# Layer 2's first five tiles scheduled ahead of layer 1's chosen-row MLP

## The chip, the cores and the metric

The kernel runs on one core of one Trainium2 chip. The metric is the device time of one execution in microseconds, as the median of several runs. Beside it stands one profiled execution, whose trace is what every row below is taken from.

## The reference

Two identical layers run one after the other on x of shape 2048 x 512 (bf16). Each layer adds a sliding-window attention and then a "mixture of depths" step that runs an MLP for a single row:

```python
x = x + A(layernorm(x))
    # qkv = x @ wqkv (512 x 1536); 32 heads of 16; query i sees keys i-255..i
    # p = softmax(q k^T / 4, masked);  (p @ v) @ wo (512 x 512)
x = x + B(layernorm(x))
    # r = x @ w_r                  one score per row, 2048 of them
    # idx = the row with the largest r (C = 1)
    # y = (silu(x[idx] @ w_gate) * (x[idx] @ w_up)) @ w_down   (512->1792->512)
    # y = y * sigmoid(r[idx]);  row idx gets + y, every other row gets + 0
    # B returns x + that update
```

So layer 2 differs from a plain second pass in one row only, and which row that is is known only when all rows of layer 1 are done. Attention looks backward alone: a query needs keys of at most 255 rows before it. With the inputs of this case the reference picks row 1105 in layer 1 (score 4.315; the next is row 1082 with 4.040). In tiles of 128 rows both lie in tile 8.

## The kernel before

The 2048 rows are 16 tiles of 128. For every tile `ln_tile` normalises (bn_stats on DVE, the rest on POOL), a DMA transpose turns the tile (`transpose`; PE does it for tiles 0 and 1 of a layer), and `proj` makes q, k and v in PSUM bank 7 (`BK_PR`), from which DVE copies them. `attend` runs eight head groups: scores on PE into banks 0 to 2 or 3 to 5 (L665, and L684 for a mask), one exp on ACT (L696; tile 0 of a layer has smaller ones, L691 and L693), an edge mask on POOL (L706, L710), and the product with v on PE into bank 6 (L725). `norm_half` divides, `out_tile` multiplies with wo in bank 7 (L750), adds the residual and calls `mod_tile`, which makes the row statistics and the score r.

After tile 15 `mod_global` finds the largest score over all rows: reductions on DVE, two matmuls with an identity (L818, L820) that turn a column into a row, a copy of the chosen tile by ACT with an index read from memory (`pick`, L836, L837), a gather by PE (L842, L844), gate and up on PE (224 matmuls, L866), silu on ACT and DVE, down on PE (L882), and the scaled result in YBC (L885). Layer 2 starts with `upd_tile` (L912): for each of its tiles DVE adds YBC times a one-hot column to the 128 rows, which changes at most one row of one tile.

No engine order is written by hand. A list scheduler (`Sched`) simulates the five engines with a cost for each operation and a priority, and emits each engine's instructions in the order so found, with semaphores. `Fast.build` gives layer 2 priorities that begin 8 tiles behind layer 1's, and each of its tiles reads what `mod_global` wrote. `warm` adds matmuls of the lowest priority (L907) that the scheduler puts where PE has nothing else: 60 after layer 1, 40 after layer 2. All users of bank 7 keep the order in which the program adds them.

At the end every engine loads a flag (L1111) that tells whether an exp over- or underflowed, and branches (L1112): the code of a slow safe version (`Safe`) lies between the branch and the end of the program. SP then waits for all DMAs (L322).

Of the kernel before, what the change touches and what calls it, by code (L numbers as in the profile page):

```python
# [57 lines left out]
class _Op:  # L58
    __slots__ = ("idx", "eng", "fn", "deps", "dur", "name", "is_dma", "prio", "signals", "count",
                 "dma_sem", "start", "end", "waits", "dma_extra", "soft")  # L60

    def __init__(self, idx, eng, fn, deps, dur, name, is_dma, prio):
# [15 lines left out]
        self.soft = ()  # L78


class Sched:
    ENGS = ("pe", "act", "dve", "pool", "sp")

    def __init__(self, dma_latency=1500.0, sem_latency=120.0, n_dma_slots=40):
# [8 lines left out]
        self._vc_lookup = {}  # L93

    def add(self, eng, fn, reads=(), writes=(), dur=100.0, name="", is_dma=False, prio=None, extra_deps=()):
# [27 lines left out]
        op.soft = soft  # L123
        self.ops.append(op)
# [25 lines left out]
    def schedule(self):  # L150
# [6 lines left out]
        remaining = [len(op.deps) for op in ops]  # L157
        ready_time = [0.0] * n
        now = {e: [] for e in self.ENGS}
        fut = {e: [] for e in self.ENGS}  # L160
        for op in ops:
            if remaining[op.idx] == 0:
                _heappush(now[op.eng], (op.prio, op.idx))
        t_eng = {e: 0.0 for e in self.ENGS}
        order = {e: [] for e in self.ENGS}
        done = 0
        while done < n:
            best = None
            for e in self.ENGS:
# [6 lines left out]
                if nw:  # L176
                    cand = (te, nw[0][0], nw[0][1], e, True)
                elif f:
                    cand = (f[0][0], f[0][1], f[0][2], e, False)
                else:  # L180
                    continue
                if best is None or cand[:3] < best[:3]:
                    best = cand
            st, p, i, e, from_now = best
            if from_now:
                _heappop(now[e])
            else:
                f = fut[e]
                nw = now[e]
                while f and f[0][0] <= st:  # L190
                    rt, p2, i2 = _heappop(f)
                    _heappush(nw, (p2, i2))
                p, i = _heappop(nw)
# [7 lines left out]
            for u in users[i]:  # L201
                remaining[u] -= 1
                rt = op.end + (0.0 if i in ops[u].soft else self.sem_latency)
                if rt > ready_time[u]:
                    ready_time[u] = rt
                if remaining[u] == 0:
                    ue = ops[u].eng
                    if ready_time[u] <= t_eng[ue]:
                        _heappush(now[ue], (ops[u].prio, u))
                    else:  # L210
                        _heappush(fut[ue], (ready_time[u], ops[u].prio, u))
        self.order = order
        self.makespan = max(op.end for op in ops) if ops else 0.0
        self.busy = {e: sum(ops[i].dur for i in order[e]) for e in self.ENGS}

# [80 lines left out]
    def run_engine(self, e, handle, sems, dma_sems):  # L296
        ops = self.ops
        for i in self.order[e]:
# [4 lines left out]
            if op.signals:  # L303
# [4 lines left out]
                else:  # L308
                    last.then_inc(sems[e], 1)

# [28 lines left out]
class Fast:  # L339
    PRE = "f_"  # L340
    RV = 2
    warm0 = 21
    warmn = (60, 40)
# [20 lines left out]
    def alloc(self):  # L364
# [42 lines left out]
        self.IDXS = self.sb("IDXS", [1, 2], I32)  # L407
# [16 lines left out]
    def alloc_attn(self):  # L424
# [8 lines left out]
        self.VSCR = self.nc.dram_tensor(self.PRE + "vscr", [self.SEQ, 544], BF16)  # L433

    def bank(self, b):
        return self.PS[:, b, :]

# [135 lines left out]
    def transpose(self, dst, dk, src, sk, tb):  # L573
# [4 lines left out]
        bb = self.bank(tb).bitcast(BF16)  # L578

        def tr(e):  # L580
# [4 lines left out]
        S.add("pe", tr, reads=sk + ["idb"], writes=["bank%d" % tb], dur=260, name="ptr")  # L585
        S.add("dve", lambda e: e.tensor_copy(out=dst, in_=bb[:, 0:512].rearrange("p (k t) -> p k t", k=4)), reads=[], writes=["bank%d" % tb, dk],  # L586
              dur=430, name="evt")

    def proj(self, L, m, banks=(BK_PR, BK_PR, BK_PR)):
# [13 lines left out]
        def pq(MB=banks[0]):  # L603
            bk = "bank%d" % MB
            for s in range(4):
                S.add("pe", lambda e, s=s: qg(e, MB, 0, s), reads=["xnt%d" % k2, "wqkv0"], writes=[bk], dur=225, name="qproj")
            for h in range(2):
                S.add("dve", lambda e, h=h: e.tensor_copy(out=self.QT[64 * h:64 * h + 64, k2, h],  # L608
                                                          in_=self.bank(MB)[64 * h:64 * h + 64, 0:512].rearrange("p (s t) -> p s t", s=4)),
                      reads=["qz%d" % k2], writes=[bk, "qt%d_%d" % (k2, h)], dur=690, name="evq")  # L610

        def pk(MB=banks[1]):
            bk = "bank%d" % MB
            for s in range(4):
                S.add("pe", lambda e, s=s: qg(e, MB, 1, s), reads=["xnt%d" % k2, "wqkv1"], writes=[bk], dur=225, name="kproj")
# [568 lines left out]
```

## Time and profile before

| | |
|---|---|
| median of 3 runs | 443.31 us (443.02 to 444.98) |
| the profiled execution, its own time | 441.75 us |
| span of the profile, first to last instruction | 440.0 us |
| PE busy | 396.6 us (90%); the filler of L907 is 23.2 us of it |
| DVE, ACT, POOL busy | 299.7, 268.8, 249.6 us |
| mean granted TensorE clock | 0.972 of full speed |

The span leaves out 1.75 us that the execution's own time holds. A busy PE is not the same as a PE that works on the result: the filler of L907 counts as busy. The engines' busy times are averages over two long even stretches (layer 1 and layer 2) and a stretch between them in which the engines take turns.

### The profile page before, as it was taken

What the parts mean: (1) busy time and instruction counts of PE and PEld (TensorE: products, weight loads), DVE (VectorE), ACT (ScalarE), POOL (GpSimd) and SP (SyncE); (2) the same over time, 40 slices, a digit from 0 to 9 for tenths busy, and PEclk for the clock granted to TensorE, in tenths of its full rate; (3) what the DMA queues carried; (4) which work ended last, traced back from release to release, by engine and by line L of the source; (5) the groups of instructions that cost most, each with busy time, mean ns of one, the idle gap of its engine ahead of it and who ended that gap; (6) DMA issues with size and microseconds to landing.
All of it is one profiled execution on the core that took longest, in us unless ns stands there. A gap on an engine that the chain in (4) does not pass through costs nothing.

```text
span 440.0 us, 17737 instructions
## 1 busy us (share of the span) xinstructions
PE 396.6 (90%) x7801; PEld 344.1 (78%) x7861; DVE 299.7 (68%) x740; ACT 268.8 (61%) x280; POOL 249.6 (57%) x468
## 2 busy tenths in 40 slices
PE   6799999999999999999558989999999999999961
PEld 2588888888888888865347878889888988998551
DVE  6899886766666656444489998874875676663730
ACT  1278777777777777830007757777668777779100
POOL 6577666666655555542076666756666555555410
PEclk9899999999999999999969999999999999999985
DMA  8543433333434332210003234222232332221000
GB/s 271 148 87 63 105 73 84 87 85 88 87 88 88 88 80 72 62 37 1 1 12 77 54 52 63 63 65 64 58 71 63 40 68 67 64 54 31 13 16 8
DMA packets 70918, 29.69 MB, mean 67 GB/s; under 512 B 51504, under 2 KB 70832, under 8 KB 70832
## 3 DMA queue, kind: packets, MB, share of 16 engines
q1 hardware_dynamic: 68576, 26.24, 27.3%
q10 hardware_dynamic: 2256, 2.23, 1.6%
q8 instruction: 64, 1.05, 1.1%
q14 instruction: 22, 0.18, 0.2%
HBM read 14.29 MB, written 6.55 MB: 47 GB/s over the span
## 4 chain that ended last, share of the span: by engine, by line
PE 71%; DVE 18%; ACT 4%; DMA 2%; issue 2%; POOL 1%; ACTq 0%; DVEq 0%; POOLq 0%
PE f_PS L665 23%; PE f_PS L725 17%; PE f_PS L599 11%; PE f_PS L750 6%; PE f_PS L907 5%; DVE f_KT L619 4%; PE f_PS L627 4%; DVE f_QT L608 3%; ACT f_PT L696 3%; DVE f_ST L560 2%; DVE f_KTN L616 2%; DVE f_xres L912 1%; PE f_PS L866 1%; PE f_PS L684 1%; DMA f_xin<-in_A_x_dram 1%
## 5 line engine op out<-in xcount | busy, mean ns | idle before, releaser
L696 ACT ACTIVATE f_PT<-f_PS 128x1152 bf16<-128x1152 f32 x240 | 256.4, 1132 | 81.1 <-PE f_PS L665 80.5
L665 PE MATMUL f_PS<-f_QT,f_KT 128*128 128x128 bf16 (+3 forms) x2976 | 173.1, 205 | 7.8 <-ACT f_PT L693 3.2
L665 PEld LDWEIGHTS f_PS<-f_QT,f_KT 128*128 128x128 bf16 x2976 | 145.8, 97 | 25.6 <-ACT f_PT L696 16.7
L706 POOL TENSOR_TENSOR f_PT<-f_PT,f_TM 128x384 bf16<-128x384 bf16 x112 | 102.5, 915 | 87.7 <-ACT f_PT L696 86.8
L725 PE MATMUL f_PS<-f_VBD,f_PT 128*128 128x68 bf16 x2880 | 120.2, 197 | 0.6 <-DVE f_ONORM L739 0.5
L725 PEld LDWEIGHTS f_PS<-f_VBD,f_PT 128*128 128x128 bf16 x2880 | 106.4, 98 | 8.2 <-issue 0.9
L599 PE MATMUL f_PS<-f_XNT,f_wqkv 128*128 128x128 bf16 x1024 | 72.5, 224 | 3.9 <-DVE f_MV L561 2.3
L599 PEld LDWEIGHTS f_PS<-f_XNT,f_wqkv 128*128 128x128 bf16 x1024 | 60.9, 100 | 4.7 <-issue 2.5
L684 PE MATMUL f_PS<-f_BM,f_II 128*128 128x64 bf16 (+1 forms) x256 | 48.8, 191 | 0.0
L737 DVE RECIPROCAL f_RDA<-f_PS 128x16 f32<-128x16 f32 x64 | 15.8, 247 | 47.2 <-PE f_PS L725 46.9
L619 DVE TENSOR_SCALAR f_KT<-f_KTN,f_KM 128x512 bf16<-128x512 bf16 x128 | 46.3, 423 | 0.8
L608 DVE CAST f_QT<-f_PS 64x512 bf16<-64x512 f32 x64 | 44.0, 687 | 4.0 <-PE f_PS L599 1.2
L627 PE MATMUL f_PS<-f_wqkv,f_XNT 128*128 128x512 bf16 x102 | 29.9, 379 | 2.6 <-DVE f_XNT L586 1.3
L750 PE MATMUL f_PS<-f_wo,f_OT 128*128 128x512 bf16 x98 | 26.3, 379 | 5.7 <-DVE f_QT L608 2.2
L691 ACT ACTIVATE f_PT<-f_PS 128x288 bf16<-128x288 f32 x16 | 6.0, 408 | 38.8 <-PE f_PS L665 38.8
L630 DVE CAST f_VN<-f_PS 128x512 bf16<-128x512 f32 x32 | 21.9, 686 | 8.8 <-PE f_PS L627 8.5
L616 DVE CAST f_KTN<-f_PS 128x512 bf16<-128x512 f32 x32 | 22.1, 689 | 8.2 <-PE f_PS L599 8.0
L739 DVE TENSOR_TENSOR f_ONORM<-f_PS,f_RDA 128x256 bf16<-128x256 f32 x64 | 27.0, 421 | 1.0
L684 PEld LDWEIGHTS f_PS<-f_BM,f_II 128*128 128x128 bf16 x256 | 24.5, 96 | 0.0
L772 POOL TENSOR_SCALAR f_RSM<-f_xres 128x1 f32<-128x1 f32 x32 | 8.0, 251 | 28.6 <-DVE f_xres L766 27.8
L562 POOL TENSOR_SCALAR f_MV<-f_MV 128x1 f32<-128x1 f32 x32 | 7.4, 232 | 29.2 <-DVE f_MV L561 26.0
L907 PE MATMUL f_PS<-f_wqkv,f_wo 128*128 128x512 bf16 x97 | 23.2, 379 | 0.2
(125 smaller groups left out, 370.1 us busy)
## 6 DMA issues: line engine op xcount, KB each, us to landing
f_vscr<-f_VN SPq DMA_DIRECT2D x32, 136.0 KB, 2.0
f_VBD<-f_vscr SPq DMA_DIRECT2D x128, 34.0 KB, 2.3
out_dram<-f_OUTB SPq DMA_DIRECT2D x16, 128.0 KB, 1.9
f_xin<-in_B_w_down_dram SPq DMA_DIRECT2D x14, 128.0 KB, 2.3
f_wg<-in_B_w_gate_dram SPq DMA_DIRECT2D x7, 256.0 KB, 3.4
f_wu<-in_B_w_up_dram SPq DMA_DIRECT2D x7, 256.0 KB, 3.6
f_wqkv<-in_A_wqkv_dram ACTq DMA_DIRECT2D x3, 512.0 KB, 5.9
f_xin<-in_A_x_dram SPq DMA_DIRECT2D x1, 1024.0 KB, 10.8
```

The lines of the kernel that those rows point to most:

```text
L599: r = e.matmul(self.bank(MB)[:, 128 * s:128 * s + 128], lhsT=self.wqkv[:, kc, off:off + 128], rhs=self.XNT[:, k2, kc, :], start=(kc == 0), ...
L608: S.add("dve", lambda e, h=h: e.tensor_copy(out=self.QT[64 * h:64 * h + 64, k2, h], in_=self.bank(MB)[64 * h:64 * h + 64, 0:512].rearrange ...
L616: S.add("dve", lambda e: e.tensor_copy(out=self.KTN[:, k2], in_=self.bank(MB)[:, 0:512].rearrange("p (s t) -> p s t", s=4)), reads=[], wri ...
L619: S.add("dve", lambda e, hh=hh: e.tensor_scalar(out=self.KT[:, k4, :, :, hh, :].rearrange("p s b k -> p (s b) k"), in0=self.KTN[:, k2].rea ...
L627: return e.matmul(self.bank(MB)[:, 0:512], lhsT=self.XNT[:, k2, kc, :], rhs=self.wqkv[:, kc, 1024:1536], start=(kc == 0), stop=(kc == 3))
L665: return e.matmul(self.bank(st + k)[:, off:off + n], lhsT=self.KT[:, (b // 4) % 4, s, b % 4].rearrange("p h k -> p (h k)"), rhs=self.QT[:, ...
L684: r = e.matmul(self.bank(st)[:, lo:192], lhsT=self.II[:], rhs=self.BM[:, lo - 128:64], start=False, stop=True, skip_group_check=True)
L696: S.add("act", lambda e: e.activation(out=view, in_=self.PS[:, st:st + 3, 0:384], func=ACTF.Exp, scale=0.25), reads=["ptz%d" % k2], writes ...
L706: S.add("pool", lambda e: e.tensor_tensor(out=w, in0=w, in1=self.TM[:].unsqueeze(1).broadcast_to([128, 6, 2, 32]), op=ALU.mult), reads=["t ...
L725: r = e.matmul(self.bank(BK_PV)[:, c0:c0 + 68], lhsT=self.PT[:, k2, p0:p0 + 128], rhs=self.VBD[:, (b // 4) % 4, b % 4].rearrange("p h (g c ...
L750: return e.matmul(self.bank(MB)[:, 0:512], lhsT=self.OT[:, ko, kc, :], rhs=self.wo[:, kc, :], start=(kc == 0), stop=(kc == 3))
L907: S.add("pe", lambda e: e.matmul(self.bank(5)[:, 0:512], lhsT=self.wo[:, 0, 0:128], rhs=self.wqkv[:, 0, 0:512], start=True, stop=True, ski ...
```

## The change

Layer 2's tiles 0 to 4 (`AHEAD = 5`) no longer read the result of layer 1's MLP: they run on the rows as they stand before the update, and their priorities follow directly on layer 1's. `mod_global(0)` gets a priority amid layer 2's first tiles and uses bank 7 alone, in short pieces (gate and up in halves of seven columns that DVE copies out, down in pieces of four). One dynamic update then changes the chosen row, if it lies in tiles 5 to 15. At that point every engine waits for the update, loads a second flag and branches: if the chosen row lay in tiles 0 to 4, a copy of those tiles, which layer 1 saved to memory, is read back, the update is applied, and all that layer 2 had done so far is done again. The scheduler now chooses the order of bank 7's users itself, each user (matmuls and the copies that read them) being one indivisible turn. The filler after layer 1 is gone. The branch at the end goes through a short block with a hint to its target ahead of it.

```diff
@@ class Sched
+    def trans(self, bank):
+        self.tr_bank.append(bank)
+        self.tr_ops.append([])
+        return len(self.tr_bank) - 1
...
@@ def schedule
+        owner = {b: None for b in self.tr_bank}
+        def blocked(i):
+            t = ops[i].tr
+            return t is not None and owner[self.tr_bank[t]] not in (None, t)
...
+    def cut(self, t):
+        self.cut_at = {}
+        for e in self.ENGS:
+            k = 0
+            while k < len(self.order[e]) and self.ops[self.order[e][k]].start < t:
+                k += 1
+            self.cut_at[e] = k
+
+    def replay(self, first, layer):
+        R = Sched(self.dma_latency, self.sem_latency, 16)
+        first(R)
...
+        keep = sorted((i for i in before if self.ops[i].layer == layer), key=lambda i: (self.ops[i].start, i))
...
@@ class Fast
-    warmn = (60, 40)
+    AHEAD = 5
+    warmn = (0, 40)
+    def hold(self, b):
+        if b != BK_PR:
+            return "bank%d" % b, None
+        t = self.S.trans(b)
+        return "bank%d.%d" % (b, t), t
...
@@ def mod_tile, L == 0
+            if m < self.AHEAD:
+                S.dma("sp", lambda e: e.dma_start(self.XSCR[rows, :], x), reads=[xk], writes=["xscr%d" % m], nbytes=262144, name="x2b", dur=650)
...
@@ def mod_global
+        side = L == 0 and self.AHEAD > 0
+        def place(b):
+            if not side:
+                return self.bank(b), "bank%d" % b, None
+            k, t = self.hold(BK_PR)
+            return self.bank(BK_PR), k, t
...
+        if side:
+            lim = float(self.SEQ - 128 * self.AHEAD - 1)
+            S.add(D, lambda e: e.tensor_scalar(out=self.FLAG[0:1, 1:2], in0=PM[0:1, 3:4], scalar1=lim, scalar2=None, op0=ALU.is_gt), ...
+            S.add(D, lambda e: e.tensor_scalar(out=self.IDXS[0:1, 2:3], in0=self.IDXS[0:1, 1:2], scalar1=self.AHEAD, scalar2=None, op0=ALU.max), ...
+            S.add(D, lambda e: e.tensor_reduce(out=self.OHL[:], in_=self.ONEHOT[:, self.AHEAD:NT], axis=AX.X, op=ALU.max), ...
...
+        if side:
+            for i, (nm, w, wk) in enumerate(ws):
+                for j0 in range(0, NF, 7):
+                    b, k, t = place(0)
+                    for j in (j0, j0 + 4):
+                        S.add("pe", lambda e, w=w, b=b, j=j, j1=min(j + 4, j0 + 7): gu(e, w, b, j, j1), ...
+                    S.add(D, lambda e, b=b, i=i, j0=j0: e.tensor_copy(out=GU[:, i, j0:j0 + 7], in_=b[:, j0:j0 + 7]), ...
...
+            for j in range(0, NF, 4):
+                j1 = min(j + 4, NF)
+                S.add("pe", lambda e, j=j, j1=j1: down(e, j, j1), reads=["ht"] + wdk, writes=[yk], dur=(j1 - j) * 216, name="down", tr=yt)
...
+            if side:
+                def upd(e):
+                    v = e.value_load(self.IDXS[0:1, 2:3], min_val=self.AHEAD, max_val=NT - 1)
+                    x = self.xres[:, bass.ds(v, 1), 0:512].rearrange("p o c -> p (o c)")
+                    return e.scalar_tensor_tensor(out=x, in0=self.YBC[:], scalar=self.OHL[:], in1=x, op0=ALU.mult, op1=ALU.add)
+                S.add(D, upd, reads=["ybc", "ohl", "idxl", "flag1"], writes=["x%d" % m for m in range(self.AHEAD, NT)], dur=1700, name="upd")
...
+    def again(self, R):
+        for m in range(self.AHEAD):
+            R.dma("sp", lambda e, m=m: e.dma_start(self.xres[:, m, 0:512], self.XSCR[128 * m:128 * m + 128, :]), ...
+            self.upd_tile(m, R)
...
@@ def ln_at
+        if L == 1 and not self.AHEAD:
+            self.upd_tile(m)
+        self.ln_tile(L, m, (7, 3)[m] if m < 2 and (L == 0 or not self.AHEAD) else None)
...
@@ def build (Fast), one loop over n = 0..31
+        def ln(n): ... S.prio_base = (n - 2.4) * ST
+        def prj(n): ... S.prio_base = (n - 0.8) * ST
+        def fin(n): ... S.prio_base = (n + 1.3) * ST
+            if n == NT:
+                S.layer = 0
+                S.prio_base = (n + 0.6) * ST
+                self.mod_global(0)
...
+LEAD = {"pe": 4, "act": 2, "dve": 8, "pool": 2, "sp": 1}
...
+            upd_op = fs.ops[[o.idx for o in fs.ops if o.name == "upd"][-1]]
+            fs.cut(upd_op.end + 200.0)
...
         def body(e, h):
-            fs.run_engine(e, h, fsem, fdma)
-            h.wait_ge(fsem[flag_op.eng], flag_op.count)
-            v = h.value_load(flag[0:1, 0:1], min_val=0, max_val=128)
-            with h.If(v):
+            fs.run_engine(e, h, fsem, fdma, 0, fs.cut_at[e])
+            h.wait_ge(fsem[upd_op.eng], upd_op.count)
+            v = h.value_load(flag[0:1, 1:2], min_val=0, max_val=1)
+            h.br_cond(v, "redo_" + e, "rest_" + e)
+            with part("rest"):
+                n = len(fs.order[e]) - LEAD[e]
+                fs.run_engine(e, h, fsem, fdma, fs.cut_at[e], n)
+                hint = h.mark_branch_hint_location()
+                fs.run_engine(e, h, fsem, fdma, n)
+                h.wait_ge(fsem[flag_op.eng], flag_op.count)
+                v = h.value_load(flag[0:1, 0:1], min_val=0, max_val=128)
+                h.br_cond(v, "safe_" + e, "pass_" + e)
+            with part("pass"):
+                h.br("done_" + e).branch_hint(hint)
+            with part("redo"):
+                fs.wait_cut(h, fsem, fdma)
+                rs.run_engine(e, h, rsem, rdma)
+                rs.wait_all(h, rsem, rdma)
+                h.br("rest_" + e)
+            with part("safe"):
...
```

## Rows read from the trace of the kernel before

**Rows 1.** The page: busy time; 40 slices of 11 us (tenths busy)

```profile
PE 396.6 (90%) x7801; PEld 344.1 (78%) x7861; DVE 299.7 (68%) x740; ACT 268.8 (61%) x280; POOL 249.6 (57%) x468
...
PE   6799999999999999999558989999999999999961
...
ACT  1278777777777777830007757777668777779100
...
PEclk9899999999999999999969999999999999999985
```

**Rows 2.** Windows: tiles 1 to 14 of each layer (stretch, busy us, count)

```profile
25.36:182.30 156.94, 153.30 (x3285) 139.09 (x3310) 112.94 (x279) 119.11 (x113) 100.62 (x184) 1.00 0.38 85
237.00:399.40 162.40, 155.02 (x3288) 140.64 (x3312) 122.57 (x283) 119.96 (x113) 99.31 (x178) 1.00 0.31 60
```

**Rows 3.** Timeline of ACT around the layer change (start us, us)

```profile
230.25 0.41 ACT L691 ACTIVATE f_PT<-f_PS 128x288 bf16<-128x288 f32 x1 [19.48 <-PE f_PS L665]
...
237.10 1.12 ACT L696 ACTIVATE f_PT<-f_PS 128x1152 bf16<-128x1152 f32 x1
```

**Rows 4.** Chain that ended last, 180 to 250 us (start us, us)

```profile
193.21 0.78 PE f_PS L725 x24
...
196.15 0.86 PE f_PS L750 x4
197.01 4.53 PE f_PS L907 x21
201.55 0.22 PE f_PS L818 x2
...
202.20 0.22 PE f_PS L820 x2
...
203.77 2.10 PE f_PS L907 x9
205.87 0.12 PE f_PS L842 x2
205.99 1.86 PE f_PS L844 x8
...
209.17 2.79 PE f_PS L866 x112
...
212.59 2.98 PE f_PS L882 x13
...
215.59 0.76 DVE f_YBC L885
...
216.38 1.42 DVE f_xres L912 x2
...
224.17 0.61 PE f_PS L583 x4
```

**Rows 5.** Windows: the MLP stretch, and ten microseconds later on

```profile
197.05:218.00 20.95, 17.81 (x183) 11.15 (x183) 8.76 (x31) 1.01 (x3) 2.65 (x6) 1.00 0.01 2
220.00:230.00 10.00, 6.29 (x53) 4.88 (x55) 7.84 (x17) 0.00 (x0) 7.97 (x15) 0.66 0.00 0
```

**Rows 6.** All lines, by instruction group: DVE's update of the residual

```profile
L912 DVE SCALAR_TENSOR_TENSOR f_xres<-f_YBC,f_ONEHOT,f_xres 128x512 f32<-128x512 f32 x16 | 12.5, 799 | 0.0
```

**Rows 7.** Lines 836, 1111, 1112 and 322: register loads, branches, final waits

```profile
L836 ACTq TENSOR_LOAD <-f_IDXS x2: 283/380/477, 203.9 to 421.7; - x2
...
L1111 PEldq TENSOR_LOAD <-flag x1: 484/484/484, 430.6 to 430.6; - x1
...
L1112 PEldq COMPARE_BRANCH  x1: 3382/3382/3382, 431.5 to 431.5; - x1
...
L1112 SPq COMPARE_BRANCH  x1: 58/58/58, 433.7 to 433.7; - x1
...
L322 SPq EVENT_SEMAPHORE  x20: 17/28/28, 438.4 to 439.6; - x20
...
L1092 SPq EVENT_SEMAPHORE  x1: 17/17/17, 440.0 to 440.0; - x1
```

**Rows 8.** DMA issues: KB each, median us to landing

```profile
f_vscr<-f_VN SPq DMA_DIRECT2D x32, 136.0 KB, 2.0
...
f_XNT<-f_XN SPq DMA_TRANSPOSE x28, 3.1
...
out_dram<-f_F4B SPq DMA_DIRECT2D x1, 1.0 KB, 2.9
```

More of the change, by code (lines that the diff above doesn't have):

```diff
@@ L59 @@
     __slots__ = ("idx", "eng", "fn", "deps", "dur", "name", "is_dma", "prio", "signals", "count",
-                 "dma_sem", "start", "end", "waits", "dma_extra", "soft")
+                 "dma_sem", "start", "end", "waits", "dma_extra", "soft", "tr", "keys", "layer")
     def __init__(self, idx, eng, fn, deps, dur, name, is_dma, prio):
@@ L78, in __init__ @@
         self.soft = ()
+        self.tr = None
+        self.keys = ()
+        self.layer = 0
 class Sched:
@@ L123, in add @@
         op.soft = soft
+        op.keys = (tuple(reads), tuple(writes))
+        op.layer = self.layer
+        op.tr = tr
+        if tr is not None:
+            self.tr_ops[tr].append(idx)
         self.ops.append(op)
@@ L157, in schedule @@
         remaining = [len(op.deps) for op in ops]
+        after = {}
+        for t in range(len(self.tr_ops)):
+            mine = set(self.tr_ops[t])
+            ext = set()
+            for i in mine:
+                ext |= ops[i].deps - mine
+            for i in mine:
+                if ops[i].eng == "pe":
+                    for d in ext - ops[i].deps:
+                        after.setdefault(d, []).append(i)
+                        remaining[i] += 1
         ready_time = [0.0] * n
@@ L160, in schedule @@
         fut = {e: [] for e in self.ENGS}
+        owner = {b: None for b in self.tr_bank}
+        left = {}
+        free_at = {b: 0.0 for b in self.tr_bank}
+        last = {b: None for b in self.tr_bank}
+        parked = {b: [] for b in self.tr_bank}
         for op in ops:
@@ L175, in schedule @@
                     _heappush(nw, (p, i))
[L176 to L180, printed above, removed]
+                while True:
+                    while nw and blocked(nw[0][1]):
+                        p, i = _heappop(nw)
+                        parked[self.tr_bank[ops[i].tr]].append(i)
+                    if nw:
+                        cand = (te, nw[0][0], nw[0][1], e)
+                        break
+                    if not f:
+                        cand = None
+                        break
+                    rt = f[0][0]
+                    while f and f[0][0] <= rt:
+                        r2, p, i = _heappop(f)
+                        _heappush(nw, (p, i))
+                    if rt > te:
+                        te = rt
+                if cand is None:
                     continue
+                if te > t_eng[e]:
+                    for (p, i) in nw:
+                        _heappush(f, (te, p, i))
+                    nw[:] = []
                 if best is None or cand[:3] < best[:3]:
                     best = cand
[L184 to L193, printed above, removed]
+            assert best is not None, "no operation can start"
+            st, p, i, e = best
+            f = fut[e]
+            nw = now[e]
+            while f and f[0][0] <= st:
+                rt, p2, i2 = _heappop(f)
+                _heappush(nw, (p2, i2))
+            p, i = _heappop(nw)
             op = ops[i]
@@ new lines, in mod_global @@
+        mb, mk, mt = (tb, tk, tt) if side else place(1)
+        mo = 128 if side else 0
+        S.add("pe", lambda e: e.matmul(tb[:, 0:128], lhsT=PM[:, 0:1].broadcast_to([128, 128]), rhs=self.IDF[:], start=True, stop=True, skip_group_check=True),
+              reads=["pm0", "idf"], writes=[tk], dur=300, name="am", tr=tt)
+        S.add("pe", lambda e: e.matmul(mb[:, mo:mo + 128], lhsT=PM[:, 1:2].broadcast_to([128, 128]), rhs=self.IDF[:], start=True, stop=True, skip_group_check=True),
+              reads=["pm1", "idf"], writes=[mk], dur=300, name="am", tr=mt)
@@ L835, in pick @@
+        S.add(D, lambda e: e.tensor_reduce(out=self.OHP[:], in_=self.ONEHOT[:], axis=AX.X, op=ALU.max), reads=["onehot"], writes=["ohp"], dur=180, name="am")
         def pick(e):
@@ L862, in gu @@
+        S.add(D, lambda e: e.reciprocal(out=SG[:, 2:3], in_=SG[:, 1:2]), reads=["sg1"], writes=["sg2"], dur=160, name="am")
         def gu(e, w, bk, j0, j1):
```

371 lines of the change are left out of this document (268 added, 103 removed).

## The prediction

> **What bounds the kernel now.** I read the page first, for the busy shares and the slices [rows 1]. PE is at 9 tenths in nearly all of them, ACT at 7 to 8, with one hole: in slices 18 to 20 ACT is at 3, 0, 0 and 0 tenths while PE still shows 9 in two of them. That is the change of layers, and PE's nines there are filler. The windows come second [rows 2]: from the first full exp of tile 1 to the first of tile 15 (14 tiles, 112 full exps) layer 1 takes 156.94 us, with PE busy for 153.30, ACT for 119.11 and DVE for 112.94. So a tile costs 11.2 us, PE sets it, and DVE needs 8.1 us of it. Layer 2 needs 162.40 us for the same tiles: PE is busy for only 1.7 us more, DVE for 9.6 more. PE waits there a little more often, and the DVE work that only layer 2 has is the update of L912, 12.5 us in all [rows 6].
>
> Third, the chain of waits across the hole [rows 4]: the last product of layer 1's attention ends at 193.99 us, the score of the last tile is known near 201 us, the MLP runs through PE, DVE and ACT in turn until YBC stands at 216.35, and layer 2's first transposes that lead on to the projections stand at 224.17. In between PE does 0.22 + 0.22 + 0.12 + 1.86 + 2.79 + 2.98 = 8.2 us of MLP. The other pieces of PE there are filler (4.53 and 2.10 are the longest) and one output projection (0.86). So each layer is PE-bound, and between them lie about 37 us that are bound by the length of a dependency chain.
>
> **The change part by part.**
>
> *The hole.* Tile 15 of layer 1 starts its exps at 182.3 [rows 2]. If layer 2 follows without a break, its tile 0 comes 11.2 us later and tile 1 another 6.85 us later, which is what tile 0 takes now from its first small exp (230.25) to tile 1's first full one (237.10) [rows 3]. So tile 1 comes at 200.4 instead of 237.1: **-36.7**.
>
> *The MLP's PE work* was hidden in the hole; now it stands among layer 2's own matmuls on the engine that sets the pace: **+8.2** [rows 4]. No engine gives this back.
>
> *Is there enough cover?* Tiles 0 to 4 are 6.85 + 4 x 11.2 = 51.7 us of work, with the MLP about 60. Counted from tile 0's start at 193.5, the chain's first matmul comes 8 us in (201.55), YBC's use 14.8 us after that (216.38), and from the use to layer 2's first exp go 13.9 us (230.25) with idle engines [rows 3, 4]. That makes 37 of 60, so 23 us of slack for waits behind other work. I cost the cover at nothing; without it PE would stand still for what is missing.
>
> *The chain's returns to PE.* PE runs in order, and at each of the MLP's returns (818, 842, 866, 882, and each half of gate and up) it waits if DVE or ACT is late. Nothing in the trace shows this mixture. Below, nothing: the scheduler had put filler into the same places and can put attention there. Above, the non-MLP time between 201.55 and 212.59, some 6 us, and once more half of that when DVE is shared, since DVE's 31 instructions of this stretch [rows 5] each may stand behind a longer one: 9. I take **+2.5**, nearer to the lower end, because PE has 52 us of other work to put there.
>
> *The point where all engines meet.* Each engine waits for the update, loads the flag and branches. PE's load takes 0.48 us, and with the steps after it the branch stands 0.9 us after the load's start (430.6 to 431.5) [rows 7]. Behind PE's wait queue the next scores, behind which ACT; SP's transposes and v stores queue behind its own wait, and the next projections wait for those (3.1 us to land [rows 8]). From below 0.9 us, as PE's work before the cut reaches to the end of the update by the scheduler's own reckoning. From above 0.9 + 3.4 for the branch, which on PE took 3382 ns at the end [rows 7], + 3.4 because PE's clock could halve: it fell after PE had run dry at 215.57, and the stretch from 220 shows a granted 0.66, which is 6.8 us at 1.2 GHz instead of 2.4 [rows 4, 5]. I take **+1.5**: the code that normally follows comes directly behind the branch.
>
> *DVE.* Sixteen updates of 0.8 us become one, with a register load of the kind of L836 (0.28 to 0.48 us) ahead of it; four copies of gate and up and three tiny operations come in. DVE loses some 10 us net [rows 6]. If that is what made layer 2 5.5 us longer than layer 1 [rows 2], it comes back: between 0 and -5.5, I take **-4**, as the extra wait lies where the updates lie.
>
> *Five copies of x2 to memory* (256 KB each) enter SP's queue, each behind POOL's scaling of its tile. Transposes and v stores queue behind them. A v store of 136 KB lands in 2.0 us [rows 8]; layer 1's early tiles could lose up to 0.8 us each, 4 in all, if SP stood waiting for POOL. I take 0: the cover is PE's queue, a tile deep. The free order of bank 7 I also cost at 0 in the even stretches, where PE is busy for 153.3 of 156.9 us and no more than 3.6 can be won or, by the same kind of waits, lost.
>
> *The end.* SP takes the branch at 433.7 and its first visible wait stands at 438.4; 20 waits take until 439.6, and the program ends at 440.0 [rows 7]. The branch jumps over the whole safe version; on PE the same one took 3.38 us. With the hint ahead of it the waits could start near 434 and end when the last row's store has landed, 2.9 us after its issue a microsecond ahead of the branch [rows 8]. Between 0 and -3.7; I take **-3.3**.
>
> On jumps the Trainium skill (Runtime: NRT & Kernel Launch, Instruction fetch mechanics) says that a taken branch whose target is not in the current two-page window forces a fetch before execution goes on, and calls run-time control flow expensive for that reason. The trace agrees at the end (3.38 us on PE). By that rule the end gains only if the hint is taken, and the middle costs another 3.4 us on every engine if its target counts as outside the window; it is rival B below.
>
> **Sum:** -36.7 + 8.2 + 2.5 + 1.5 - 4 - 3.3 = **-31.8 us**. The profiled execution took 441.75 us with a span of 440.0, so it would take about 410.0. The median of the runs lies 1.56 us above that execution: 443.31 - 31.8 = **411.5 us**.
>
> **Rivals.**
>
> *A, the chain outlasts its cover.* If each of DVE's 31 instructions waits behind one of up to 0.8 us, the chain grows by some 25 us, to the 23 us of slack, and with waits on PE's side by 8 more. PE then runs out of tiles ahead of tile 5 and stands still for 2 to 10 us: 414 to 421. For it: one handoff after another, each on an engine that is 70% busy. Against it: every part of the MLP has a priority above tiles 1 to 4, and typical waits are half an instruction.
>
> *B, the branches miss.* Fetches of 3.4 us in the middle, and the hint doesn't help at the end: 411.5 + 3.4 + 3.3 = 418. For it: the only branch in the trace cost this on every engine. Against it: the middle's target lies next in the code.
>
> *C, layer 2 does not get ahead.* The tiles are there to run, but some queue (SP's transposes, bank 7's turns, bank 4, which tile 15's last transpose uses) holds them until the MLP is through. Then only the end and DVE's relief remain, 443.3 - 3.3 - 4 = 436. Against it: nothing that tile 0 reads comes later than its own rows.
>
> *D, slower: the replay is taken.* Its place is the branch in the middle, its condition a chosen row below 640. Then 52 us of tiles run twice, with a refill of 14 us (216.38 to 230.25) and five reads: 411.5 + 52 + 14 + some 8 = 485. What decides is the row alone; the reference picks 1105, and its six best candidates all lie in tiles 5 to 9.
>
> **How the numbers follow.** The forecast with its bounds (406.5 with every term at its good end) has a chance of 0.66, A 0.17, B 0.11, C 0.04, D 0.02. The range 404 to 423 holds the first three, with some room below for bubbles that go with the hole; outside it remain C, D and a few hundredths of the bad ends. Half a per cent (2.2 us) is about what a measurement tells from no change: faster 0.95 (all but D and a poor C), within 0.5% 0.02, slower 0.03.
>
> **What would show it.** The profile after should show ACT without its zeros in slices 18 to 20, L907 with about 40 instructions, the two stretches of 14 tiles both near 157 us plus the MLP's 8, L912 gone from the even stretch, one COMPARE_BRANCH per engine in the middle with under 1 us behind it, and under 4 us from the last row's store to the end. The prediction is wrong in its core if PE shows slices of 7 or less between 190 and 260 us (A, or PE held at the returns), if the middle branch has a gap of over 3 us behind it (B), or if tile 1's first full exp of layer 2 comes later than 215 us.

## The result and the profile after

The kernel after takes 417.35 us (median of 4 runs, 416.10 to 420.34) beside 444.14 us for the kernel before (443.02 to 445.25) on the same chip. The ratio is 0.9407, with a 95% interval of 0.9345 to 0.9468: faster by 26.8 us, where 31.8 were forecast. The profiled execution took 416.46 us with a span of 414.7. (In the rows PE is TensorE, PEld its weight loads, DVE VectorE, ACT ScalarE, POOL GpSimd and SP SyncE; a q behind a name means the engine's sequencer, which waits, reads registers and branches.)

The page of the kernel after (busy time, then 40 slices of 10.4 us, in tenths), beside [rows 1]:

```profile
PE 387.0 (93%) x7793; PEld 337.4 (81%) x7793; DVE 286.0 (69%) x730; ACT 271.1 (65%) x280; POOL 249.3 (60%) x468
...
PE   6899999999999999999899899999999999998960
...
ACT  1178768877777777776775378777787778777000
PEclk9799999999999999999999999999999999999965
```

ACT's three empty slices (19 to 21) are gone; the lowest between the layers is 3. PE is still at 8 or 9 nearly throughout, but now with attention: its filler (L1138) fell to 40 matmuls, all of them after 382 us.

The windows of the kernel after, beside [rows 2]: tiles 1 to 14 of layer 1, then the same 14 tiles of layer 2, cut at the first full exp of tile 3 (stretch, then busy us and count of PE, PEld, DVE, ACT, POOL, granted clock, DMA share, GB/s):

```profile
25.00:181.60 156.60, 155.56 (x3326) 139.75 (x3325) 116.99 (x289) 119.22 (x114) 109.23 (x202) 1.00 0.42 94
...
200.40:235.90 35.50, 32.21 (x640) 28.07 (x639) 21.76 (x69) 20.33 (x26) 12.55 (x24) 1.00 0.20 38
235.90:371.60 135.70, 134.42 (x2834) 120.99 (x2833) 99.14 (x238) 103.92 (x97) 91.33 (x163) 1.00 0.28 60
```

Layer 1's stretch is what it was (156.60 us beside 156.94). Layer 2's tile 1 has its first full exp at 200.4 us, the very time forecast, instead of 237.1. The 14 tiles take 35.5 + 135.7 = 171.2 us; the forecast has 162.4 - 4 + 8.2 + 2.5 + 1.5 = 170.6. Two tiles carry nearly all of the MLP (35.5 us for 22.4 before), the other twelve take 11.3 us each.

What PE waits for in the first of these two stretches (what it waited for, us in all, times, longest):

```profile
PE f_PS L844 <- DVE f_QT L786: 1.5, 1, 1.5
PE f_PS L904 <- POOL f_PT L889: 0.7, 2, 0.4
PE f_PS L844 <- ACT f_PT L875: 0.6, 1, 0.6
PE f_PS L1043 <- DVE f_VN L809: 0.3, 1, 0.3
```

Only the last of these stands at one of the MLP's returns to PE (L1043 picks the row). The first is the meeting point. Its timeline, PE's rows and then DVE's (start us, us, what, idle before it):

```profile
233.05 0.55 PE L904 MATMUL f_PS<-f_VBD,f_PT 128*128 128x68 bf16 x12
235.15 0.31 PE L844 MATMUL f_PS<-f_QT,f_KT 128*128 128x32 bf16 x3 [1.54 <-DVE f_QT L786]
...
231.19 0.75 DVE L1110 TENSOR_SCALAR f_YBC<-f_PS,f_SGT 128x512 f32<-128x512 f32 x1 [1.87 <-PE f_PS L1105]
233.35 0.75 DVE L1116 SCALAR_TENSOR_TENSOR f_xres<-f_YBC,f_OHL,f_xres 128x512 f32 x1 [1.41 <-issue]
234.02 0.68 DVE L786 CAST f_QT<-f_PS 64x512 bf16<-64x512 f32 x1
```

Two things run side by side from the update's end at 234.10: DVE's cast of q, which is queued behind the update, and PE's own read of the flag with its branch. Both are over when PE goes on at 235.15. The lines of the read and of the branches (duration ns min/median/max, first and last start us):

```profile
L1114 DVEq TENSOR_LOAD <-f_IDXS x1: 554/554/554, 232.0 to 232.0; - x1
...
L1396 PEldq TENSOR_LOAD <-flag x1: 491/491/491, 234.1 to 234.1; - x1
...
L1397 DVEq COMPARE_BRANCH  x1: 55/55/55, 234.8 to 234.8; - x1
...
L1397 PEldq COMPARE_BRANCH  x1: 88/88/88, 235.0 to 235.0; - x1
```

PE's branch starts 0.86 us after its load and the next weights are loaded 0.13 us after that. So where the target lies next in the code, a branch costs 0.1 us. (The Trainium skill, Advanced Engine Details and Errata, Control Flow Timing, gives about 108 ns for a compare-and-branch; these take 40 to 88 ns, and those at the end that go to the short block, which also lies next, 84 to 139.)

The end, beside [rows 7]: the last branches, SyncE's final waits and the drain that follows on each engine:

```profile
L1407 POOLq COMPARE_BRANCH  x1: 57/57/57, 393.4 to 393.4; - x1
L1407 ACTq COMPARE_BRANCH  x1: 58/58/58, 402.0 to 402.0; - x1
L1407 PEldq COMPARE_BRANCH  x1: 361/361/361, 405.3 to 405.3; - x1
L1407 DVEq COMPARE_BRANCH  x1: 76/76/76, 406.0 to 406.0; - x1
L1407 SPq COMPARE_BRANCH  x1: 58/58/58, 407.5 to 407.5; - x1
...
L489 SPq EVENT_SEMAPHORE  x20: 17/28/28, 412.2 to 413.4; - x20
...
L1368 POOLq DRAIN  x1: 123/123/123, 396.2 to 396.2; - x1
L1368 ACTq DRAIN  x1: 89/89/89, 404.6 to 404.6; - x1
L1368 PEldq DRAIN  x1: 48/48/48, 405.7 to 405.7; - x1
L1368 DVEq DRAIN  x1: 57/57/57, 408.9 to 408.9; - x1
...
L1368 SPq COMPARE_BRANCH  x1: 53/53/53, 413.5 to 413.5; - x1
L1368 SPq DRAIN  x1: 70/70/70, 414.4 to 414.4; - x1
```

The jump, with a hint ahead of it and a short block in front, took 361 ns on PE, where it took 3382 before [rows 7]. But DVE still reaches its drain 2.9 us after its branch, ACT 2.6 and POOL 2.8 (before: 3.1, 2.5 and 2.7), and SyncE's first wait comes 4.8 us after its branch (before 4.7, 433.7 to 438.4). The last row's store is issued at 406.3, and the span ends 8.4 us later; before it was 7.4. The step that is longer here is the one from SyncE's last branch (413.5) to its drain (414.4), 0.97 us where it was 0.17. It isn't a price of the change: runs 1, 2, 3 and 8 below end with the same code, take 0.18 us at this step, and end 7.1 to 7.6 us after the store's issue.

Last, ACT at layer 2's final tile (start us, us, what, idle before it):

```profile
373.70 1.13 ACT L875 ACTIVATE f_PT<-f_PS 128x1152 bf16<-128x1152 f32 x1 [0.98 <-PE f_PS L844]
375.04 5.45 ACT L875 ACTIVATE f_PT<-f_PS 128x1152 bf16<-128x1152 f32 x5 [0.21 <-PE f_PS L844]
381.24 1.13 ACT L875 ACTIVATE f_PT<-f_PS 128x1152 bf16<-128x1152 f32 x1 [0.76 <-PE f_PS L844]
```

From the tile's start (371.6) to the end of its last exp go 10.8 us, and 9.1 before (399.5 to 408.6). Twice ACT waits for scores that stand behind an output projection on PE.

So the forecast held up to tile 15 within 0.6 us, and missed at the end: 43.1 us from tile 15's start to the end of the span, where it was 40.5 and 37.2 were forecast.

### The profile page after: what moved, and what is told of

It reads as the page before. It is cut to its first block, busy times and chain, and to the rows that moved or that the text cites. A ratio compares the mean times of both kernels' runs of the same rounds, so it can differ in the third digit from the quotient of the medians.

```text
span 414.7 us, 17705 instructions
## 1 busy us (share of the span) xinstructions
PE 387.0 (93%) x7793; PEld 337.4 (81%) x7793; DVE 286.0 (69%) x730; ACT 271.1 (65%) x280; POOL 249.3 (60%) x468
## 4 chain that ended last, share of the span: by engine, by line
PE 82%; DVE 9%; ACT 3%; DMA 2%; issue 1%; DVEq 0%; POOL 0%; ACTq 0%
PE f_PS L844 28%; PE f_PS L904 20%; PE f_PS L777 12%; PE f_PS L931 7%; PE f_PS L806 6%; ACT f_PT L875 3%; DVE f_KT L797 2%; PE f_PS L1138 2%; DVE f_QT L786 2%; PE f_PS L863 2%; PE f_PS L1068 1%; DMA f_xin<-in_A_x_dram 1%; DMA f_OT<-f_ONORM 1%; PE f_PS L1045 1%; DVE f_KTN L794 1%
## 5 line engine op out<-in xcount | busy, mean ns | idle before, releaser
L777 PE MATMUL f_PS<-f_XNT,f_wqkv 128*128 128x128 bf16 x1024 | 71.3, 222 | 3.1 <-DVE f_MV L738 2.4
L797 DVE TENSOR_SCALAR f_KT<-f_KTN,f_KM 128x512 bf16<-128x512 bf16 x128 | 43.1, 396 | 0.8
L806 PE MATMUL f_PS<-f_wqkv,f_XNT 128*128 128x512 bf16 x128 | 38.2, 389 | 0.9 <-DVE f_QT L786 0.7
L931 PE MATMUL f_PS<-f_wo,f_OT 128*128 128x512 bf16 x128 | 32.8, 379 | 1.2 <-DVE f_QT L786 0.9
L918 DVE TENSOR_TENSOR f_ONORM<-f_PS,f_RDA 128x256 bf16<-128x256 f32 x64 | 26.8, 419 | 0.9
L935 DVE TENSOR_TENSOR f_xres<-f_PS,f_xres 128x512 f32<-128x512 f32 x16 | 11.1, 692 | 17.1 <-PE f_PS L931 17.1
L948 DVE SCALAR_TENSOR_TENSOR f_JUNK<-f_xres,f_WR 128x512 bf16<-128x512 f32 x32 | 22.4, 701 | 0.0
L889 POOL TENSOR_TENSOR f_PT<-f_PT,f_TM 128x192 bf16<-128x192 bf16 x16 | 8.9, 558 | 22.4 <-ACT f_PT L872 12.3
L946 DVE BATCH_NORM_STATS2 f_ST<-f_xres 128x6 f32<-128x512 f32 x32 | 21.8, 680 | 0.6
```

Of the source, the lines that this page charges most:

```text
L777: r = e.matmul(self.bank(MB)[:, 128 * s:128 * s + 128], lhsT=self.wqkv[:, kc, off:off + 128], rhs=self.XNT[:, k2, kc, :], start=(kc == 0), ...
L797: S.add("dve", lambda e, hh=hh: e.tensor_scalar(out=self.KT[:, k4, :, :, hh, :].rearrange("p s b k -> p (s b) k"), in0=self.KTN[:, k2].rea ...
L806: return e.matmul(self.bank(MB)[:, 0:512], lhsT=self.XNT[:, k2, kc, :], rhs=self.wqkv[:, kc, 1024:1536], start=(kc == 0), stop=(kc == 3))
L918: S.add("dve", lambda e: e.tensor_tensor(out=self.ONORM[:, ko, 256 * half:256 * half + 256].rearrange("p (h d) -> p h d", d=16), in0=acc[: ...
L931: return e.matmul(self.bank(MB)[:, 0:512], lhsT=self.OT[:, ko, kc, :], rhs=self.wo[:, kc, :], start=(kc == 0), stop=(kc == 3))
```

## The experiments

All are edits of the kernel after, and each was timed against the kernel before on its own chip (443.6 to 444.7 us). Totals are medians.

**1. Layer 2 waits for the MLP again.** Layer 2's statistics wait for the MLP's result and the filler is back; the short pieces, the single update, the branches and the free order of bank 7 stay.

```diff
-        S.add("dve", ... reads=[xk], ..., name="bnst")
+        S.add("dve", ... reads=[xk] + (["ybc"] if L == 1 and self.AHEAD else []), ..., name="bnst")
...
+                self.warm(60)
+                ln(NT)
+                prj(NT)
+                ln(NT + 1)
+                prj(NT + 1)
```

> All of the change stays except the running ahead: every tile of layer 2 waits for YBC again, and the 60 fillers are back. Theory (the 27 us come from tiles 0 to 4 filling the hole): the hole is back, ACT is idle for some 35 us between the layers, and the time is 436 to 445 us. Rival (the free order of bank 7, the relief of DVE and the split MLP carry a good part): under 430 us.

442.60 us, ratio 0.9981 (0.9947 to 1.0014): without the running ahead the rest of the change gains nothing. It also prices the rest of the change. The same 14 tiles of layer 2, then tiles 1 and 2 and the remaining twelve (the columns are those of the windows above):

```profile
243.00:400.20 157.20, 155.49 (x3312) 139.00 (x3312) 108.92 (x268) 119.14 (x112) 96.55 (x172) 1.00 0.29 62
...
243.00:265.60 22.60, 21.79 (x436) 19.20 (x436) 17.88 (x42) 17.13 (x16) 12.71 (x24) 1.00 0.32 67
265.60:400.20 134.60, 133.71 (x2878) 119.81 (x2876) 91.04 (x229) 102.01 (x97) 83.84 (x148) 1.00 0.28 61
```

157.2 us for 162.4 [rows 2]: with one update instead of sixteen, DVE is busy for 108.9 us instead of 122.6 and layer 2 is as fast as layer 1. (Bank 7's free order is in this run too. Layer 1 has it as well and is unchanged, so the update is the likelier cause, but no run separates the two.) That -5.2 us is eaten by a longer hole, 61.0 us between the two tiles' starts (182.0 to 243.0) for 54.7 before. Nearly all of the difference lies ahead of the update's end (222.6 us, where it was 217.1 for the first one), and part of it is the clock: PE was granted 1.2 GHz from 210.3 to 217.1 us, and the product with w_down took 4.84 us for 2.98 before [rows 4]:

```profile
213.74 4.84 PE f_PS L1105 x14
```

Against this run, the MLP among layer 2's tiles costs 171.2 - 157.2 = 14.0 us, and the windows split it: in tiles 1 and 2 PE is busy for 32.21 - 21.79 = 10.4 us more and idle for 3.3 - 0.8 = 2.5 more; the other twelve tiles take 1.1 more. (Of the 10.4 us some 9.8 are the MLP's own matmuls.)

**2. Three tiles ahead instead of five.**

```diff
-    AHEAD = 5
+    AHEAD = 3
```

> Three tiles run ahead in place of five. From the trace of the changed kernel: tile 0's exps start near 192.9, the update ends at 234.1, and a tile that waits for it needs some 14 us more until its first exp, so cover of 55 us is needed. Tiles 0 to 2 with the MLP hold 6.9 + 22.4 + 8.2 = 37. Theory (cover is what counts, and with less of it the chain also gets shorter because there is less to queue behind): PE stands still for 10 to 18 us, 426 to 435 us. Rival (the cover was never short, three tiles do): within 2 us of 417.

429.42 us, ratio 0.9672 (0.9613 to 0.9732). PE's longest waits between 198 and 255 us:

```profile
PE f_PS L806 <- DMA f_XNT<-f_XN: 6.2, 1, 6.2
PE f_PS L904 <- DVE f_xres L935: 2.0, 1, 2.0
```

PE runs out of tiles and waits, and it is granted 1.2 GHz from 235.2 to 252.3 us (columns as in the windows above):

```profile
235.20:252.30 17.10, 8.98 (x66) 6.18 (x67) 10.56 (x28) 2.09 (x2) 11.94 (x30) 0.50 0.25 55
```

The kernel after, with five tiles, has neither: the cover is what the gain hangs on, and five are enough.

**3. No meeting point.** The wait, the flag, the branch in the middle and the replay are left out (right only while the chosen row lies in tiles 5 to 15, as here).

```diff
...
-            h.wait_ge(fsem[upd_op.eng], upd_op.count)
-            v = h.value_load(flag[0:1, 1:2], min_val=0, max_val=1)
-            h.br_cond(v, "redo_" + e, "rest_" + e)
...
```

> The wait of all engines, the flag load, the branch and the replay are left out (right only while the chosen row lies in tiles 5 to 15, as here). The trace of the changed kernel shows PE idle for 1.54 us there and 1.7 us of lost matmul pitch. Theory (the meeting point costs what PE stands still, and no more): -1.5 us, 415.9. Rival (draining all five queues costs more than the gap on PE, since ACT and SP have to catch up afterwards): -3 to -6 us.

418.05 us, ratio 0.9424 (0.9366 to 0.9482): nothing gained. PE's standstill is still there, with DVE's cast of q now its only cause:

```profile
236.99 0.31 PE L844 MATMUL f_PS<-f_QT,f_KT 128*128 128x32 bf16 x3 [1.17 <-DVE f_QT L786]
```

Neither theory nor rival was right. The read of the flag and the branch are not free, but they lie beside DVE's queue and hide behind it, all but 1.54 - 1.17 = 0.4 us.

**4. Less of the MLP's work on PE.** Layer 1's MLP leaves out three of four matmuls for gate and up and 10 of the 14 with w_down.

```diff
-                for kc in range(4):
+                for kc in range(4 if L else 1):
...
-                for j in range(j0, j1):
+                for j in range(j0, j0 + 1):
...
```

> Layer 1's MLP leaves out PE work: one of four matmuls for each column of gate and up (56 of 224 remain), and 4 of 14 in the product with w_down, 4.2 us of PE time less; the chosen row comes out different. The order of all instructions stays. Theory (PE sets the pace, so the MLP's PE work adds in full): -4.2 us, near 413. Rival (what costs there is the waits between the MLP's steps, and PE's work hides in them): under 1.5 us less.

414.65 us, ratio 0.9360 (0.9299 to 0.9421). The 14 tiles take 168.4 us (200.26 to 368.64) instead of 171.2: of 4.2 us of matmuls taken away, 2.8 come back. So PE does set the pace there, but not for every microsecond; part of the rest turned into waits: PE's idle time in the 14 tiles grew by 0.9 us (168.38 - 162.93 beside 171.20 - 166.63).

**5. No branches and no safe version.** Everything from the meeting point on is one straight line, with neither replay nor safe version.

```diff
-            h.wait_ge(fsem[upd_op.eng], upd_op.count)
...
-            nc.switch_bb("done_" + e)
+            fs.run_engine(e, h, fsem, fdma, fs.cut_at[e])
```

> No branch at all: the middle one and the replay are left out, and so are the last flag load, the last branch and the safe version (its check of over- and underflow decides nothing any more). In the trace of the changed kernel SP takes the last branch at 407.5 and its first visible wait stands 4.8 us later. Theory (that gap is the fetch of code behind a far jump, and the hint did not help SP): without the jump the end comes 3.4 us or more earlier, 412 to 414 us, and the stretch from the last row's store to the end falls from 8.3 us to under 5. Rival (SP waits for the last store to land or for the other engines): that stretch stays within 1 us.

414.59 us, ratio 0.9337 (0.9283 to 0.9391). The store is issued at 408.28 and the span ends at 411.87: 3.6 us instead of 8.4. So the 4.8 us that are gone hang on the branch, and under 4 us is what the store itself needs.

**6. The hints stand further ahead.**

```diff
-LEAD = {"pe": 4, "act": 2, "dve": 8, "pool": 2, "sp": 1}
+LEAD = {"pe": 12, "act": 4, "dve": 24, "pool": 8, "sp": 6}
```

> The hint to the last branch's target stands earlier in each engine's code: PE 12 operations ahead in place of 4, ACT 4 (2), DVE 24 (8), POOL 8 (2), SP 6 (1). In the changed kernel only PE passed the jump quickly (0.36 us against 3.38 before), while DVE, ACT, POOL and SP stood for 2.5 to 4.8 us as before. Theory (their hints came too late): SP's gap falls below 2 us and the time by 3. Rival (the hint does nothing on these engines, wherever it stands): gaps and time as before, within 0.5 us.

417.92 us, ratio 0.9408 (0.9353 to 0.9463). SyncE's branch and its waits:

```profile
L1407 SPq COMPARE_BRANCH  x1: 58/58/58, 409.4 to 409.4; - x1
...
L489 SPq EVENT_SEMAPHORE  x20: 17/28/28, 414.1 to 415.3; - x20
```

Still 4.7 us, and DVE, ACT and POOL also as before (2.9, 2.6 and 2.8). It wasn't the lead: PE's jump takes 450 ns here, and the other four show no effect of the hint at either distance. Even on PE the hint's part is not isolated, since no run has the short block without a hint, and it isn't certain: PE's jump took 356 to 450 ns in ten of the twelve traces that have a hint, but longer in runs 1 and 4:

```profile
L1412 PEldq COMPARE_BRANCH  x1: 1537/1537/1537, 432.1 to 432.1; - x1
...
L1407 PEldq COMPARE_BRANCH  x1: 2190/2190/2190, 403.3 to 403.3; - x1
```

**7. One final wait instead of twenty.** SyncE waits for the last store alone.

```diff
-                fs.wait_all(h, fsem, fdma, engines=False)
+                last = fs.ops[fs.dma_ops[-1]]
+                h.wait_ge(fdma[last.dma_sem], last.count)
```

> SP's last waits, one for each of 40 DMA counters, become one for the last row's store alone, which itself was issued behind all other stores. Theory (the 4.8 us behind SP's branch are 3.4 us of fetch and 20 waits that the trace doesn't show, and 20 more follow in 1.2 us): the end comes 2.0 to 2.5 us earlier. Rival (the waits stand in the shadow of the store's landing): less than 0.5 us.

416.18 us, ratio 0.9374 (0.9319 to 0.9429); in the trace store to end falls from 8.4 to 6.1 us. The size is the theory's, its reason was not: from SyncE's branch (407.34) to the next one (411.90) still go 4.6 us with one wait between them, so the jump itself is that long, and the 20 waits that the trace shows (1.2 us) come on top. A further 0.8 us is the step from the last branch to the drain, 0.18 us here, which varies between runs of the same end. In the medians only 1.2 us are left, with overlapping intervals.

**8. Nine tiles ahead: the replay is taken**, since the chosen row 1105 lies in tile 8.

```diff
-    AHEAD = 5
+    AHEAD = 9
```

> Nine tiles run ahead in place of five. The chosen row lies in tile 8, so the middle branch goes to the replay: what the prediction's rival D prices at 485 us. From the trace of the changed kernel tiles 0 to 2 and part of tile 3 are done when the branch comes at 235, 40 us after tile 0's start; they would run again, with a refill, five to nine reads back, and code fetched from afar: 470 to 495 us. If the replay cost less than 20 us, the branch would pay even for rows in the first tiles: under 440.

491.66 us in a single execution (rival D had 485). PE's branch in the middle, taken to code that lies far off:

```profile
L1397 PEldq COMPARE_BRANCH  x1: 3754/3754/3754, 234.1 to 234.1; - x1
```

The same branch that costs 88 ns when its target lies next costs 3754 ns here, without a hint. (So the rule of the Trainium skill, Runtime: NRT & Kernel Launch, Instruction fetch mechanics, that a taken branch out of the window forces a fetch, agrees with this trace; the page gives no price.)

**9. The last projections later.** Those of tiles 13 and 14 of layer 2 get a place behind tile 15's scores.

```diff
-            S.prio_base = (n + 1.3) * ST
+            S.prio_base = (n + 1.3 if n < K - 3 or n == K - 1 else K - 0.75 if n == K - 3 else K - 0.25) * ST
```

> The output projections of layer 2's tiles 13 and 14 get a later place in the order, behind the scores of tile 15; nothing else changes. Theory (a part of the missing time is the order of the last tiles): the stretch from tile 15's first exp to the end of the last exp falls from 10.8 us towards the 9.1 of before, since ScalarE no longer waits twice (0.98 and 0.76 us) for scores that stand behind a projection: -1.0 to -1.7 us in the span. Rival (TensorE is the bound there in any order, and the projections are only paid later, ahead of the second feed-forward): the last exp ends earlier, the last product with V does not, and the total stays within 0.5 us.

417.56 us, ratio 0.9376 (0.9343 to 0.9409). In the trace the theory holds for its stretch, 9.5 us instead of 10.8:

```profile
371.87 5.44 ACT L875 ACTIVATE f_PT<-f_PS 128x1152 bf16<-128x1152 f32 x5 [1.03 <-PE f_PS L844]
377.92 5.45 ACT L875 ACTIVATE f_PT<-f_PS 128x1152 bf16<-128x1152 f32 x5 [0.61 <-PE f_PS L844]
```

The second feed-forward's result (F4B) also comes 32.4 us after tile 15's start instead of 33.6, so the 1.2 us are not paid back behind it, as the rival had it. In the total they can't be told from the spread of the runs. Part of that spread goes with the clock: this execution shows a stretch of 3.4 us at 1.2 GHz from 224.7 us on, while PE is busy, which the profile after has not:

```profile
224.70:228.10 3.40, 3.40 (x78) 3.40 (x75) 0.66 (x4) 0.73 (x1) 1.94 (x4) 0.50 0.33 82
```

Three profiles with one such stretch between 217 and 229 us take 172.4 to 172.7 us for the 14 tiles (runs 3, 6, 9), four without it 171.05 to 171.2 (the kernel after, runs 5, 7 and 11). What brought the clock down in some executions stays open.

**10. The register load moved.** DVE reads the tile index for the update two steps earlier.

```diff
+        def ht(e):
+            if side:
+                tile["v"] = e.value_load(self.IDXS[0:1, 2:3], min_val=self.AHEAD, max_val=NT - 1)
+            return e.tensor_tensor(out=self.HT[:], in0=U, in1=E[:, 1, :], op=ALU.mult)
...
-                    v = e.value_load(self.IDXS[0:1, 2:3], min_val=self.AHEAD, max_val=NT - 1)
-                    x = self.xres[:, bass.ds(v, 1), 0:512].rearrange("p o c -> p (o c)")
+                    x = self.xres[:, bass.ds(tile["v"], 1), 0:512].rearrange("p o c -> p (o c)")
```

> The register load of the chosen tile's index moves from VectorE's update of the chosen row to an operation two steps earlier, so that less stands ahead of the next tile's cast of q. Theory (TensorE's standstill of 1.5 us near 235 is VectorE's queue: load, update, cast): the standstill falls by about the 0.9 us of the load, to 0.3 to 0.7 us, and the total by 0.5 to 1.2 us. Rival (the load only stands somewhere else in the same chain, and the chain as a whole is what TensorE waits for): the standstill stays at 1.3 to 1.6 us, total unchanged.

418.87 us, ratio 0.9405 (0.9366 to 0.9443): nothing gained; this profile, too, has a stretch at 1.2 GHz (3.4 us from 219.4). YBC's start to the end of the update, 2.9 us in the kernel after, is 2.0:

```profile
233.28 0.75 DVE L1116 TENSOR_SCALAR f_YBC<-f_PS,f_SGT 128x512 f32<-128x512 f32 x1 [1.87 <-PE f_PS L1111]
234.55 0.75 DVE L1121 SCALAR_TENSOR_TENSOR f_xres<-f_YBC,f_OHL,f_xres 128x512 f32 x1 [0.52 <-DVE f_YBC L1116]
...
236.40 0.56 PE L904 MATMUL f_PS<-f_VBD,f_PT 128*128 128x68 bf16 x12 [1.09 <-DVE f_ST L737]
```

But PE still stands still for 1.09 us, although products with V, which no cast holds up, come next there: from the update's end (235.30) to 236.40 it reads the flag and branches. With run 3 this settles the meeting point: two waits of 1.1 to 1.2 us lie side by side, and taking away either leaves the other. Taking away both wasn't tried.

**11. SyncE jumps before it stores.** Its flag and branch come ahead of the last row's store, which moves behind the jump with the final waits.

```diff
-                hint = h.mark_branch_hint_location()
-                fs.run_engine(e, h, fsem, fdma, n)
+                if e != "sp":
+                    hint = h.mark_branch_hint_location()
+                    fs.run_engine(e, h, fsem, fdma, n)
...
+                with part("tail"):
+                    fs.run_engine(e, h, fsem, fdma, n)
+                    fs.wait_all(h, fsem, fdma, engines=False)
+                    h.br("done_" + e)
```

> SyncE's last read of the flag, and its branch, come ahead of the store of the chosen row and of the final waits, which stand behind the jump; so the jump's 4.8 us run while SyncE would only wait for the second feed-forward's last result. Theory (the end is long because SyncE's fetch at the jump stands between store and end): store to end falls from 8.4 us to 3.5 to 4.5, the total by 4 to 4.6 us, to about 413. Rival (something else ends last: another engine's jump of 2.6 to 2.9 us, or the store's own way to memory): the end falls by less than 2.5 us, and the chain ends on another engine.

414.13 us, ratio 0.9309 (0.9272 to 0.9347). SyncE's branch, its jump, its store and its final waits:

```profile
L1408 SPq COMPARE_BRANCH  x1: 34/34/34, 394.3 to 394.3; - x1
...
L1411 SPq COMPARE_BRANCH  x1: 38/38/38, 394.3 to 394.3; - x1
...
L1134 SPq DMA_DIRECT2D out_dram<-f_F4B x1: 362/362/362, 406.1 to 406.1; - x1
...
L491 SPq EVENT_SEMAPHORE  x20: 17/28/28, 406.5 to 409.6; - x20
```

SyncE takes the jump (L1411) at 394.3 us, while it would only wait for the row until 405, and store to end takes 4.3 us instead of 8.4: -4.1 in the trace, -3.2 in the medians. The waits now end when the store has landed, 3.5 us after its issue.

**12. Runs 9, 10 and 11 together.** The diff is those three.

> The three edits together: the projections of tiles 13 and 14 later, the index load earlier, SyncE's jump ahead of its store. Theory (each stands at another place of the chain that ends last, so they add): -5 to -7 us, about 411 us. Rival (only the end counts, the other two are taken up by TensorE's work): no more than the jump alone, -4 to -4.6 us, about 413 us.

414.45 us, ratio 0.9316 (0.9283 to 0.9348): as the rival had it, no more than the jump alone. The tail's 1.3 us are there (9.5 us), and so is the short end (4.4), but the 14 tiles take 172.2 us without any stretch at the lower clock, 1.0 more than in the kernel after. Moving the load has changed the order in which DVE and POOL work from 234 to some 306 us, in run 10 as here; that this costs the 1.0 us is not shown by itself. Run 11 has the lowest ratio, but its lead over the kernel after (0.9309 to 0.9407) is small beside the two intervals.

## Why the prediction was right, point by point

*The hole, -36.7:* right; tile 1 came at 200.4 us. That it fits to the tenth is luck: layer 1's tile 15 started 0.8 us earlier than before (181.6 for 182.4), and from there to tile 1 went 18.8 us where 11.2 + 6.85 = 18.05 were reckoned. Runs 1 and 2 show that the gain hangs on this.

*DVE's relief, -4:* run 1 measures 5.2, if all of it is DVE's.

*The MLP among layer 2's tiles, 8.2 + 2.5 + 1.5 = 12.2:* 14.0 by run 1. PE's added work was 10.4 rather than 8.2; some 9.8 us of it are the MLP's own matmuls, which by run 4 do set the pace, though only for about two thirds of them. The waits at the MLP's returns to PE, where the 2.5 were put, came to 0.3; 1.3 us more stood at attention's own handoffs (POOL, ACT). With -5.2 for -4, the two misses nearly cancel: 171.2 for 170.6.

*The meeting point, +1.5:* right in size, 1.54, and the lower bound's 0.9 us from load to branch was there. Left out was the second wait beside it, DVE's queue of load, update and cast (runs 3 and 10). Rival B's fetch in the middle didn't come, because the target lies next; run 8 shows it where it doesn't.

*The copies to memory and bank 7's order, 0:* layer 1's stretch is unchanged (156.6 for 156.9), and run 1, which keeps both, is as fast as before. They paid for nothing in themselves.

*The end, -3.3:* this is the step that failed. The hint was believed for every engine, from PE's price alone; PE's jump got short (3382 to 361 ns) and that of SyncE, which ends the program, did not (4.8 us after 4.7). Runs 5, 6, 7 and 11 show that SyncE's jump is the price, that a longer lead doesn't help, and that jumping earlier does. That the 4.6 to 4.8 us are spent fetching code is the likely reading, but no run looks into them. Half of rival B thus came true. In the profiled execution store to end was 1.0 us longer than before, 0.8 of it the step at the last branch, which varies between runs (0.2 to 1.0 us) and whose cause stays open. And a loss that no term had: tile 15's order, 1.7 us, of which run 9 gives back 1.3. Together +2.6 for -3.3, or 5.9 us, against a total miss of 416.46 - 410.0 = 6.5.

*The rivals:* A didn't come: the chain took 27 us from the last score to the update (207.3 to 234.1), some 16 before, and no tile ran out; run 2 shows its form when cover is short. B counted for itself that the branch at the end cost 3.4 us on every engine; before the change it was 2.5 (ACT) to 4.7 us (SyncE). C's price was not met by run 1, which has its form (442.6 for 436): the end gave nothing and the relief of 5.2 us went into the hole. D's was near, at 491.7 for 485, with nine tiles and in a single execution.

## What to carry to other kernels

A hole between two pace-bound stages that is a dependency chain can be filled by running the next stage ahead on data that will hardly change; here its length came back in full because the cover exceeded the chain with its waits, and the chain's own work was then paid on the engine that sets the pace. Where every engine must meet, look for what lies beside the wait as well: two waits of equal length hide each other when only one of them is taken away (runs 3 and 10). Put a jump over much code where its engine would wait anyway, and take the price of a jump from the engine that ends the program.

## What the runs showed of the hardware

A jump over the safe version cost each engine its own price, from the branch to the next row: PE 3.4 us in the kernel before, and over all the runs that have the jump ahead of the final waits DVE 2.8 to 3.2, ACT 2.5 to 2.9, POOL 2.6 to 3.0, SyncE 4.1 to 4.8. With a hint ahead of it and a short block in front PE took 0.36 to 0.45 us in ten of twelve traces (1.5 in run 1, 2.2 in run 4); the other four engines showed no effect, at either of two distances. A conditional branch to the code that lies next took 40 to 88 ns on the five engines in the middle of the kernel after, and 84 to 139 ns at its end.
